# V' on eight small TensorE tiles, a cosine by one shifted sine, and other durations in the planner: a fused Nyström-attention and two-MLP kernel

## The chip, the cores and the metric

The program runs on one core of a Trainium2 chip, in one launch. The metric is the device time in microseconds (us). Three runs of the kernel before took 878.0, 874.71 and 877.42 us; their median is 877.42.

## The reference

Attention has 4 batches, 8 heads, 576 positions and 64 dimensions, with 32 landmarks per head (m). Its output, as 2304 tokens of 512 numbers, goes through two MLPs.

```python
q_lm, k_lm = segment means of q, k            # 32 per head
A, Bm, C = sm(q, k_lm), sm(q_lm, k_lm), sm(q_lm, k)
Z = Bm.T / (norm1 * norminf + 1e-6)
for _ in range(6):
    Z = 2 * Z - Z @ Bm @ Z
x = (A @ Z @ C @ v)                           # 2304 x 512
h = x @ w_in;  x = (h * cos(h)) @ w_out       # 512 -> 2048 -> 512
h = x @ w_in2; out = (max(h, 0) + alpha * min(h, 0)) @ w_out2
```

## The kernel before

**Algebra and tiles.** The first MLP's w_in is folded into the attention: per batch, W = Z C v (32 x 64 per head) is multiplied with w_in to V' = W w_in, and then h = A V'. Eight heads are four pairs p; two pairs make half c of a batch (c is 0 or 1), so V' is, per batch b, per block fb of 512 columns of w_in and per half c, one tile of 128 rows (4 heads of 32 landmarks) by 512. `vprime` (line 864) makes it: two matmuls in plain float32 (L885), each over all 128 rows (two heads of 64 dimensions) and 64 weight columns, the second on the other 64 columns of the array. The weights are block-diagonal: `put` (L857) writes W for both heads of a pair and multiplies what belongs to the other head with a mask of zeros. One ScalarE copy (L887) rounds V' from PSUM to its high part, one VectorE subtraction (L888) makes the low part. There are 4 x 4 x 2 = 32 such steps, here taken two by two (c = 0, 1) as 16 pairs.

**Ticks.** `tick` (line 909) is one block of 288 tokens by 128 columns of h, 128 in all. Six matmuls (L925) make h in one of two PSUM banks "h"; then the chain is ACT k = round(h/2pi) (L930), DVE u = h/2pi - k (L932), ACT sin(pi u) (L934), ACT square, times 2 (L935), DVE (1 - u)·h, which is h cos h (L936), ACT rounding to gh (L939), POOL or DVE gl (L940, by the helper at L323), and twelve matmuls (L952) into four banks "acc". The bank "h" is free again after L936.

**What else runs.** `unit` (line 523) makes A and C v of a half, `z_path` (line 757) the iteration for Z of a batch, both with the two PSUM banks "x" from the second batch on. `convert` (line 456) turns a float64 weight tile into float32 by three DVE operations (L467, L469, L471) after a load into one of three slots "raw". The second MLP (`btick`, `strassen`: L1238, L1319, L1283) follows the ticks, from about 460 us on.

**Order.** Nothing is ordered by hand. `Plan.go` (line 114) walks through all operations with an estimated duration of each (`pe`, `act`, `dve`, `pool`, lines 296 to 309), due times (`target`) and free buffers, picks what starts first, and so fixes the order on every engine; an operation that may run on two engines goes to the one that would end it first. Each engine then runs its list in that order, whatever the chip's real durations are.

Of the kernel before, what the change touches and what calls it, by code (L numbers as in the profile page):

```python
# [9 lines left out]
F32 = mybir.dt.float32  # L10
# [248 lines left out]
def kernel(  # L259
# [48 lines left out]
    def pool(n):  # L308
        return ("POOL", n / 480.0 + 0.15)
# [122 lines left out]
    kq = [view([P, 2, 2, 2, M], F32)(at_kq + 32 * M * p) for p in range(NP)]  # L432
# [3 lines left out]
    alpha_sb = keep.tile([P, NF], F32, name="alpha_sb")  # L436
    kqb = [[g.buf(None) for _ in range(2)] for _ in range(NP)]
# [85 lines left out]
    def unit(u, tu):  # L523
# [72 lines left out]
        if m == 0:  # L596
            pt = bank(1)
            for i, nm in enumerate(("kn", "qn")):
                a = nat[nm]
                if (KN["LM"] >> (2 * u + i)) & 1:  # L600
                    ls = atb(0, "ls", [P, P])
                    op(dve(1152), lambda e, a=a, ls=ls: nc.vector.tensor_reduce(
                        ls.t.rearrange("p (h d) -> p h d", h=2),
                        a.t.rearrange("p (h r d) -> p h d r", h=2, d=D), axis=AX.X, op=ALU.add), r=[a], w=[ls])
# [13 lines left out]
                op(pe(NR * P, 4), lm, r=[a], w=[pl])  # L618
                ls = atb(0, "ls", [P, P])
                op([act(128), dve(128)], lambda e, ls=ls, pl=pl: copy(e, ls.t[0:64], pl.t[0:64, 0:P]),  # L620
                   r=[pl], w=[ls])
                op(pe(128, 2), lambda e, i=i, ls=ls: nc.tensor.transpose(
                    pt.t[:, i * P:i * P + 64], ls.t[0:64], ident[0:64, 0:64]), r=[ls], w=[pt])
            for hh in range(2):
                sl = slice(64 * hh, 64 * hh + 64)

                def kw(e, sl=sl, hh=hh):
                    o = kq[p][sl, :, :, hh, :]
                    i = pt.t[sl, 0:256].rearrange("p (x y b m) -> p x y b m", x=2, y=2, b=2)[:, :, 0]
                    if e == "ACT":  # L630
                        nc.scalar.activation(o, i, AF.Copy, scale=1.0 / (8.0 * SEG))
                    else:
                        nc.vector.tensor_scalar_mul(o, i, 1.0 / (8.0 * SEG))
                op([dve(128), act(128)], kw, r=[pt], w=[kqb[p][0], kqb[p][1]])
        else:
            for i, t in enumerate((kt, qt)):
# [15 lines left out]
                for hh in range(2):  # L652
                    sl = slice(64 * hh, 64 * hh + 64)

                    def kw(e, sl=sl, hh=hh, i=i, lt=lt):
                        o = kq[p][sl, i, :, hh, :]
# [7 lines left out]
        def scores(dst, ch, which, t, bb, pp):  # L664
# [3 lines left out]
                lhsT=kq[pp][:, which, bb].rearrange("p h m -> p (h m)"),  # L668
# [5 lines left out]
        for ch in range(2):  # L674
# [5 lines left out]
            o1 = op(pe(n, 4), cs, r=[kt, kqb[p][1]], w=[sc[ch]] if ch else sc, after=[o1] if ch else [])  # L680
# [49 lines left out]
        for ch in range(2):  # L730
# [5 lines left out]
            o1 = op(pe(n, 4), asc, r=[qt, kqb[p][0]],  # L736
# [20 lines left out]
    def z_path(b, tz):  # L757
# [12 lines left out]
        def pbm(e):  # L770
            for p in range(g0, g0 + n):
                for bb in range(2):
                    for hh in range(2):
# [3 lines left out]
                            lhsT=kq[p][64 * hh:64 * hh + 64, 1, bb, hh, :],  # L777
                            rhs=kq[p][64 * hh:64 * hh + 64, 0, bb, hh, :],
# [40 lines left out]
        w_ = sb("wt", [P, 2, P])  # L819
# [39 lines left out]
        for i in range(2):  # L859
            wt[b, i] = w_  # L860
# [3 lines left out]
    def vprime(b, fb, c, target):  # L864
        g.ctx = f"{'vV'[b > 0]}{2 * fb + c}"
        if b > 1:
            wi = []
            for p in (2 * c, 2 * c + 1):
# [6 lines left out]
        else:  # L875
            wi = [wi1[fb, 2 * c], wi1[fb, 2 * c + 1]]
        w_ = wt[b, c]
        pv = psb("x")
        d = vv[b, fb, c] = v_tile()
        valloc.append((b, fb))  # L880
# [6 lines left out]
        op(act(512, True), lambda e: nc.scalar.activation(d.t[:, 0], pv.t, AF.Copy), r=[pv], w=[d], target=target + 0.8)  # L887
        op(dve(512), lambda e: nc.vector.tensor_tensor(d.t[:, 1], pv.t, f32(d.t[:, 0]), op=ALU.subtract),  # L888
           r=[pv], rw=[d], target=target + 1.5)
# [19 lines left out]
    def tick(s):  # L909
# [9 lines left out]
        def h1_mm(e):  # L919
# [8 lines left out]
        h1op[s] = op(pe(6 * CW), h1_mm, r=[vv[b, fb, 0], vv[b, fb, 1], *ah[b, 0], *ah[b, 1]], w=[hp], target=T,  # L928
                     after=[h1op[s - 1]] if s else [])
        op(act(CW, True), lambda e: nc.scalar.activation(k_.t, hp.t[:, 0:CW], AF.Copy, scale=INV2PI),  # L930
# [16 lines left out]
        for o in range(NK):  # L947
# [9 lines left out]
            y1op[s] = op(pe(3 * CW), y1_mm, r=[wh, wl, gh, gl], target=tick_time(s + LA) + 0.1 * o, **kw)  # L957
# [34 lines left out]
    def vgroup(b, fbs):  # L992
        for fb in fbs:
            for c in range(2):
                vprime(b, fb, c, tick_time(vfirst[b, fb]) - KN["VE"])
# [226 lines left out]
    def strassen(n, i, sg, js, X, Y):  # L1222
# [8 lines left out]
        def product(x, k, A, B):  # L1231
# [11 lines left out]
            return op(pe(6 * hw), mm, r=[a_, b_], hold=[(X, Y)[k // 2]], target=T, after=gates["h2"], **kw)  # L1243
# [23 lines left out]
    def btick(n, i, sg, jj):  # L1267
# [6 lines left out]
        if w < 512:  # L1274
            H = {}
            for D, A_, B_, x in ((X, "A11", "A12", 0), (Y, "A21", "A22", 2)):
# [9 lines left out]
                gates["h2"] = [op(pe(12 * w), mm, r=[y for z in ab for y in z], w=[D], target=T,  # L1286
# [7 lines left out]
        for j, x in ((ja, 0), (ja + 2 * NSG, 2)):  # L1294
# [18 lines left out]
            for t in range(w // P):  # L1313
# [8 lines left out]
                y2op[n, i] = op(pe(3 * 512), y2_mm, r=[wh, wl, gh, gl], target=btime(n, i + 1) + 4.6, **kw)  # L1322
# [62 lines left out]
```

## Time and profile before

| what | value |
|---|---|
| profiled execution | 876.8 us, span 875.0 us |
| median of 3 runs | 877.42 us |
| busy over the span: PE, DVE, ACT, POOL | 823.1, 642.5, 475.9, 200.0 us |
| mean granted TensorE clock | 0.974 |

The span is the time from the first to the last instruction. A busy TensorE (PE) means that a matmul was in flight; weight loads (PEld) overlap it. A clock of 1.00 is 2.4 GHz, one of 0.5 is 1.2 GHz; a stretch between them had both.

### The profile page before, as it was taken

What the parts mean: (1) busy time and instruction counts of PE and PEld (TensorE: products, weight loads), DVE (VectorE), ACT (ScalarE), POOL (GpSimd) and SP (SyncE); (2) the same over time, 40 slices, a digit from 0 to 9 for tenths busy, and PEclk for the clock granted to TensorE, in tenths of its full rate; (3) what the DMA queues carried; (4) which work ended last, traced back from release to release, by engine and by line L of the source; (5) the groups of instructions that cost most, each with busy time, mean ns of one, the idle gap of its engine ahead of it and who ended that gap; (6) DMA issues with size and microseconds to landing.
All of it is one profiled execution on the core that took longest, in us unless ns stands there. A gap on an engine that the chain in (4) does not pass through costs nothing.

```text
span 875.0 us, 16117 instructions
## 1 busy us (share of the span) xinstructions
PE 823.1 (94%) x6065; PEld 721.5 (82%) x6065; DVE 642.5 (73%) x1296; ACT 475.9 (54%) x1085; POOL 200.0 (23%) x221
## 2 busy tenths in 40 slices
PE   6658899999999999998999889999999999999997
PEld 4337678889788878877899779899999999999996
DVE  5978979986986789777978999865665566555563
ACT  4357647787866678566876443443344324433431
POOL 0325402334431332122511332200220012000110
PEclk9788799999999999999999999999999999999999
DMA  9474716676266935455463322130113011310231
GB/s 234 144 200 122 180 30 219 198 181 137 89 208 200 226 101 157 165 189 169 133 207 110 112 78 85 60 105 25 37 61 86 25 37 61 85 37 25 70 111 24
DMA packets 87901, 103.28 MB, mean 118 GB/s; under 512 B 35856, under 2 KB 62992, under 8 KB 87824
## 3 DMA queue, kind: packets, MB, share of 16 engines
q1 hardware_dynamic: 87824, 102.27, 40.6%
q8 instruction: 47, 0.77, 0.4%
q14 instruction: 30, 0.25, 0.1%
HBM read 79.96 MB, written 22.28 MB: 117 GB/s over the span
## 4 chain that ended last, share of the span: by engine, by line
PE 66%; DVE 15%; DMA 10%; ACT 3%; issue 3%; SPq 1%; DVEq 0%; ACTq 0%
PE acc L1319 20%; PE acc L952 14%; PE h L1238 9%; PE h L925 7%; PE x L1238 7%; DMA m<-in_moe_w_in_dram 5%; DVE m L323 3%; DMA m<-in_moe_w_out_dram 3%; PE x L885 2%; DVE m L469 1%; PE h L1283 1%; PE x L1283 1%; DVE m L471 1%; DMA m<-wi2d 1%; DVE m L936 1%
## 5 line engine op out<-in xcount | busy, mean ns | idle before, releaser
L952 PE MATMUL acc<-m,m 128*128 128x288 f32 x1536 | 239.1, 302 | 2.7 <-DVE m L323 2.2
L323 POOL TENSOR_TENSOR m<-m,m 128x288 fp32r<-128x288 f32 (+4 forms) x126 | 125.3, 1000 | 444.6 <-ACT m L939 193.3
L952 PEld LDWEIGHTS acc<-m,m 128*128 128x128 f32 x1536 | 214.8, 191 | 13.5 <-issue 5.5
L1319 PE MATMUL acc<-m,m 128*128 128x512 f32 x864 | 207.6, 391 | 0.7 <-DVE m L323 0.4
L323 DVE TENSOR_TENSOR m<-m,m 128x512 fp32r<-128x512 f32 (+3 forms) x274 | 174.0, 659 | 30.2 <-ACT m L1160 7.4
L1319 PEld LDWEIGHTS acc<-m,m 128*128 128x128 f32 x864 | 158.9, 189 | 31.5 <-DVE m L323 0.9
L925 PE MATMUL h<-m,m 128*128 128x288 f32 x768 | 131.2, 307 | 12.5 <-DVE m L936 11.1
L925 PEld LDWEIGHTS h<-m,m 128*128 128x128 f32 x768 | 110.7, 193 | 29.1 <-DVE m L936 18.6
L1238 PE MATMUL h<-m,m 128*128 128x256 f32 x768 | 107.8, 284 | 4.0 <-ACT m L318 4.0
L1307 ACT ACTIVATE m<-m 128x512 fp32r<-128x512 f32 (+1 forms) x80 | 46.3, 588 | 111.8 <-DVE m L1305 109.4
L1238 PEld LDWEIGHTS h<-m,m 128*128 128x128 f32 x768 | 101.0, 192 | 7.1 <-ACT m L318 4.8
L1238 PE MATMUL x<-m,m 128*128 128x256 f32 x576 | 80.9, 286 | 1.8 <-ACT m L318 1.8
L939 ACT ACTIVATE m<-m 128x288 fp32r<-128x288 f32 x128 | 56.2, 441 | 45.1 <-DVE m L936 41.3
L1261 DVE TENSOR_TENSOR m<-h,m 128x512 f32<-128x512 f32 x32 | 22.1, 690 | 78.1 <-ACT m L318 77.9
L1238 PEld LDWEIGHTS x<-m,m 128*128 128x128 f32 x576 | 74.0, 191 | 3.4 <-ACT m L318 2.0
L936 DVE SCALAR_TENSOR_TENSOR m<-m,h 128x288 f32<-128x288 f32 x128 | 56.8, 445 | 24.1 <-ACT m L935 23.8
L318 ACT ACTIVATE m<-h 128x256 f32<-128x256 f32 (+3 forms) x90 | 35.5, 395 | 63.2 <-PE h L1238 57.3
L930 ACT ACTIVATE m<-h 128x288 int32<-128x288 f32 x128 | 51.8, 406 | 31.8 <-PE h L925 30.9
L934 ACT ACTIVATE m<-m 128x288 f32<-128x288 f32 x128 | 55.7, 441 | 24.0 <-DVE m L932 23.4
L1071 ACT ACTIVATE m<-m 128x512 fp32r<-128x512 f32 x68 | 41.3, 627 | 45.2 <-PE h L1238 19.0
L932 DVE SCALAR_TENSOR_TENSOR m<-h,m 128x288 f32<-128x288 f32 x128 | 57.3, 448 | 6.2 <-ACT m L930 5.5
L935 ACT ACTIVATE m<-m 128x288 f32<-128x288 f32 x128 | 55.5, 439 | 2.3
(143 smaller groups left out, 864.8 us busy)
## 6 DMA issues: line engine op xcount, KB each, us to landing
m<-in_moe_w_in_dram SPq DMA_DIRECT2D x32, 512.0 KB, 4.9
m<-wi2d SPq DMA_DIRECT2D x56, 256.0 KB, 3.2
m<-in_moe_w_out_dram SPq DMA_DIRECT2D x24, 512.0 KB, 4.7
m<-w1d SPq DMA_DIRECT2D x32, 256.0 KB, 5.7
y1d<-m SPq DMA_DIRECT2D x24, 288.0 KB, 2.9
out_dram<-m SPq DMA_DIRECT2D x36, 128.0 KB, 2.4
w1d<-m SPq DMA_DIRECT2D x16, 256.0 KB, 5.6
wi2d<-m SPq DMA_DIRECT2D x16, 256.0 KB, 2.8
```

The source lines that it names most:

```text
L323: ENG[e].tensor_tensor(o, a, b, op=ALU.subtract)
L925: nc.tensor.matmul(out=hp.t[:, 0:CW], lhsT=w_[:, js], rhs=x[:, cs], start=(i == 0), stop=(i == 5))
L930: op(act(CW, True), lambda e: nc.scalar.activation(k_.t, hp.t[:, 0:CW], AF.Copy, scale=INV2PI), r=[hp], w=[k_], target=T + 0.8)
L932: op(dve(CW), lambda e: nc.vector.scalar_tensor_tensor(u.t, hp.t[:, 0:CW], INV2PI, k_.t, op0=ALU.mult, op1=ALU.subtract), r=[hp, k_], w=[u])
L934: op(act(CW), lambda e: nc.scalar.activation(u.t, u.t, AF.Sin, scale=math.pi), rw=[u], aset="sin")
L935: op(act(CW), lambda e: nc.scalar.activation(u.t, u.t, AF.Square, scale=math.sqrt(2.0)), rw=[u])
L936: op(dve(CW), lambda e: nc.vector.scalar_tensor_tensor(hc.t, u.t, 1.0, hp.t[:, 0:CW], op0=ALU.subtract, op1=ALU.mult, reverse0=True), r=[h ...
L939: op(act(CW), lambda e: nc.scalar.activation(gh.t, hc.t, AF.Copy), r=[hc], w=[gh, gl])
L952: nc.tensor.matmul(out=yg[o].t[:, 0:CW], lhsT=w_.t[:, sl], rhs=x.t, start=(j == ja and i == 0), stop=(j == jb and i == 2),)
L1238: nc.tensor.matmul(out=rv(k), lhsT=a_.t[:, p, c2, js], rhs=b_.t[:, q_, c2, 0:hw], start=(first and c2 == 0 and i == 0), stop=(c2 == 1 and ...
L1307: op(act(w), lambda e, m_=m_, gh=gh: nc.scalar.activation(gh.t[:, 0:w], m_.t[:, 0:w], AF.Copy), r=[m_], w=[gh, gl])
L1319: nc.tensor.matmul(out=ya[n][t].t, lhsT=gv(x_), rhs=r_.t, start=(st and k == 0), stop=(en and k == 2))
```

## The change

Three edits are made together.

**V'.** `vprime` now does both halves of a block fb in one step: eight matmuls, each of 64 rows (one head's dimensions) and 32 weight columns, on eight different tiles of the array. Half c writes PSUM bank `pv[c]`; head hh of pair bb stands in rows 64·hh, and its result in partitions 32·(2·bb + (hh xor c)). Without zero blocks the mask goes, and `put` is a plain copy that DVE or ACT may do. So that A's columns stand in the same order, the landmarks `kq` change their layout, and the two heads of a pair are swapped on A's side for c = 1.

**Cosine.** k = round(h/2pi + 1/4), u = h/2pi - k, and cos(h) = sin(2pi·u + pi/2), with the quarter turn as a per-partition bias from a tile `quarter`. The square is gone; the last DVE operation is a plain product.

**Planner.** The durations that it counts with are others (PE: per column 0.4258 ns instead of 0.4202, and 9 ns per matmul instead of 5 ns per step; POOL slower; ACT a little slower from SBUF; one reduction 2.06 instead of 1.27 us). Nothing else of its rules changes.

```diff
-    def pe(n, passes=1):
-        return ("PE", n * passes / 2380.0 + 0.005)
+    def pe(n, passes=1, k=1):
+        return ("PE", n * passes * 0.4258e-3 + 0.009 * k)
     def act(n, psum=False):
-        return ("ACT", n / 1200.0 + (0.05 if psum else 0.09))
+        return ("ACT", n * 0.8e-3 + 0.07 if psum else n * 0.835e-3 + 0.11)
     def pool(n):
-        return ("POOL", n / 480.0 + 0.15)
+        return ("POOL", n / 400.0 + 0.1)
...
             def put(e, bb=bb):
-                o = w_.t[:, :, 64 * bb:64 * bb + 64].rearrange("p i (h m) -> p h i m", h=2)
-                x = pw[bb].t[:, 0:n * M].rearrange("p (o i m) -> p o i m", o=1, i=n)
-                nv.tensor_tensor(o, x.to_broadcast([P, 2, n, M]), mask.to_broadcast([P, 2, n, M]), op=ALU.mult)
-            vop(128, put, r=[pw[bb]], w=[w_], target=tz)
+                copy(e, w_.t[:, :, bb], pw[bb].t[:, 0:n * M].rearrange("p (i m) -> p i m", i=n))
+            op([dve(64), act(64, True)], put, r=[pw[bb]], w=[w_], target=tz)
...
+        pv, d = [psb("x") for _ in range(2)], [v_tile() for _ in range(2)]
         def v_mm(e):
-            for bb in range(2):
-                sl = slice(64 * bb, 64 * bb + 64)
-                nc.tensor.matmul(out=pv.t[sl], lhsT=w_.t[:, c, sl], rhs=f32(wi[bb].t))
-        op(pe(512, 4), v_mm, r=[w_, *wi], w=[pv, d], target=target)
+            for c in range(2):
+                for bb in range(2):
+                    for hh in range(2):
+                        qd = 2 * bb + (hh ^ c)
+                        sl = slice(64 * hh, 64 * hh + 64)
+                        nc.tensor.matmul(
+                            out=pv[c].t[32 * qd:32 * qd + 32], lhsT=w_.t[sl, c, bb], rhs=f32(wi[2 * c + bb].t)[sl])
+        op(pe(512, 4, 12), v_mm, r=[w_, *wi], w=[*pv, *d], target=target)
...
-        op(act(CW, True), lambda e: nc.scalar.activation(k_.t, hp.t[:, 0:CW], AF.Copy, scale=INV2PI),
+        op(act(CW, True), lambda e: nc.scalar.activation(k_.t, hp.t[:, 0:CW], AF.Copy, scale=INV2PI, bias=0.25),
...
-        op(act(CW), lambda e: nc.scalar.activation(u.t, u.t, AF.Sin, scale=math.pi), rw=[u], aset="sin")
-        op(act(CW), lambda e: nc.scalar.activation(u.t, u.t, AF.Square, scale=math.sqrt(2.0)), rw=[u])
-        op(dve(CW), lambda e: nc.vector.scalar_tensor_tensor(
-            hc.t, u.t, 1.0, hp.t[:, 0:CW], op0=ALU.subtract, op1=ALU.mult, reverse0=True), r=[hp, u], w=[hc],
+        op(act(CW), lambda e: nc.scalar.activation(u.t, u.t, AF.Sin, scale=2.0 * math.pi, bias=quarter), rw=[u], aset="sin")
+        op(dve(CW), lambda e: nc.vector.tensor_tensor(hc.t, u.t, hp.t[:, 0:CW], op=ALU.mult), r=[hp, u], w=[hc],
```

**Where it moves instructions.** In the lists below m with a number is a tile in SBUF, and h, x and acc are the PSUM banks. After the change the lines stand a little lower: L885 is L886, L925 is L930, L952 is L955, L590 is L592, L839 is L841, L743 and L749 are L745 and L751.

First place: TensorE at a V' pair in the middle of the ticks (last batch, block 2). Before:

```order
L952 MATMUL acc<-m_541,m_698 128x288 x2
L952 MATMUL acc<-m_541,m_699 128x288
L885 MATMUL x<-m_204,m_450 64x512 x2
L885 MATMUL x<-m_280,m_450 64x512 x2
L925 MATMUL h<-m_884,m_509 128x288 x3
L925 MATMUL h<-m_1189,m_578 128x288 x3
L952 MATMUL acc<-m_541,m_742 128x288 x2
```

With the change:

```order
L955 MATMUL acc<-m_555,m_709 128x288 x2
L955 MATMUL acc<-m_555,m_710 128x288
L886 MATMUL x<-m_198,m_479 32x512 x4
L886 MATMUL x<-m_235,m_479 32x512 x4
L955 MATMUL acc<-m_555,m_762 128x288 x2
L955 MATMUL acc<-m_555,m_763 128x288
L930 MATMUL h<-m_819,m_542 128x288 x3
L930 MATMUL h<-m_1173,m_543 128x288 x3
```

Four matmuls of 64 columns have become eight of 32; the place among h and acc is nearly the same.

Second place: TensorE at the second V' pair of the first batch (its half c = 0 is m_468). Before:

```order
L925 MATMUL h<-m_453,m_473 128x288
L925 MATMUL h<-m_452,m_473 128x288
L885 MATMUL x<-m_468,m_450 64x512 x2
L590 MATMUL x<-m_69,m_154 128x128 x3
L925 MATMUL h<-m_445,m_463 128x288
L925 MATMUL h<-m_446,m_463 128x288
```

With the change:

```order
L930 MATMUL h<-m_499,m_485 128x288
L930 MATMUL h<-m_498,m_485 128x288
L886 MATMUL x<-m_452,m_479 32x512 x4
L886 MATMUL x<-m_510,m_479 32x512 x4
L930 MATMUL h<-m_382,m_484 128x288
L930 MATMUL h<-m_383,m_484 128x288
```

Before, half c = 1 (m_558) came only after two more ticks' h (12 matmuls). Now both halves stand ahead of these two ticks.

Third place: DVE in the first batch's iteration for Z (its steps are the 128x192 rows). Before:

```order
L746 TENSOR_REDUCE m_172<-m_172 128x18
L839 SCALAR_TENSOR_TENSOR m_69<-m_69,h 128x192
L747 TENSOR_SCALAR m_172<-m_172 128x18
L471 SCALAR_TENSOR_TENSOR m_204<-m_154,m_204 128x512
L467 TENSOR_SCALAR m_280<-m_154 128x512
L839 SCALAR_TENSOR_TENSOR m_69<-m_69,h 128x192
L469 SCALAR_TENSOR_TENSOR m_280<-m_154,m_280 128x512
```

With the change:

```order
L751 TENSOR_TENSOR m_191<-m_191 128x576
L841 SCALAR_TENSOR_TENSOR m_69<-m_69,h 128x192
L754 STREAM_TRANSPOSE m_191<-m_191 128x576
L740 STREAM_TRANSPOSE m_191<-acc 128x320
L740 STREAM_TRANSPOSE m_191<-acc 128x256
L841 SCALAR_TENSOR_TENSOR m_69<-m_69,h 128x192
L745 TENSOR_REDUCE m_191<-m_191 128x18
L469 TENSOR_SCALAR m_235<-m_153 128x512
L841 SCALAR_TENSOR_TENSOR m_69<-m_69,h 128x192
L323 TENSOR_TENSOR m_191<-m_191 128x576
```

A multiplication and a subtraction 576 wide, which POOL did here before, stand between the steps of the iteration. In the whole program the list of DVE has five of L749's eight operations more than before, four more of the 512-wide L1099, and 14 more subtractions gl; POOL has these fewer.

## Rows read from the trace of the kernel before

**Rows 1.** The page, part 1: busy time, share and instructions of each engine.

```profile
PE 823.1 (94%) x6065; PEld 721.5 (82%) x6065; DVE 642.5 (73%) x1296; ACT 475.9 (54%) x1085; POOL 200.0 (23%) x221
```

**Rows 2.** Busy time by stage: the stage (us), its length, busy us (count) per engine.

```profile
core 0: us, PE busy (x) PEld busy (x) DVE busy (x) ACT busy (x) POOL busy (x), PEclk, DMA share, GB/s
0.00:43.00 43.00, 27.82 (x336) 18.33 (x338) 30.61 (x79) 18.25 (x37) 8.77 (x15) 0.85 0.70 188
43.00:110.00 67.00, 51.33 (x326) 39.08 (x323) 55.73 (x107) 44.55 (x99) 25.82 (x29) 0.84 0.67 168
110.00:460.00 350.00, 340.81 (x2867) 298.11 (x2867) 280.29 (x625) 249.89 (x597) 104.70 (x121) 1.00 0.56 163
460.00:540.00 80.00, 75.22 (x494) 69.87 (x494) 73.47 (x136) 38.65 (x83) 20.49 (x14) 0.96 0.31 97
540.00:870.00 330.00, 327.91 (x2050) 296.12 (x2049) 202.36 (x353) 124.32 (x272) 40.23 (x43) 1.00 0.19 57
```

**Rows 3.** The same for short stretches, columns as in rows 2.

```profile
20.00:40.00 20.00, 13.27 (x254) 8.08 (x254) 18.93 (x57) 7.93 (x19) 5.65 (x4) 0.84 0.45 129
...
490.00:500.00 10.00, 8.26 (x43) 6.34 (x41) 10.00 (x15) 4.64 (x10) 3.68 (x3) 1.00 0.27 84
...
520.00:530.00 10.00, 7.70 (x48) 7.29 (x46) 8.66 (x18) 4.13 (x9) 0.12 (x1) 0.83 0.45 134
```

**Rows 4.** Timeline of PE at a V' pair: start us, length us, line, operands, count.

```profile
131.74 0.55 PE L952 MATMUL acc<-m,m 128*128 128x288 f32 x3
132.22 1.94 PE L885 MATMUL x<-m,m 128*64 128x512 f32 x8
134.09 1.06 PE L925 MATMUL h<-m,m 128*128 128x288 f32 x6
```

**Rows 5.** Line L885 from 100 to 425 us: duration ns min/median/max, first and last start.

```profile
L885 PE MATMUL x<-m,m x112: 592/592/643, 126.2 to 419.2; 128*64 128x512 f32 x112
```

**Rows 6.** Timeline of PE: steps on tiles of 64 and 32 rows by 32 columns.

```profile
239.09 0.33 PE L775 MATMUL x<-m 64*32 64x32 f32 x16
...
248.73 0.53 PE L826 MATMUL x<-m 32*32 32x96 f32 x16
```

**Rows 7.** Timeline of PE at the start: V' of the first batch; in brackets idle before, releaser.

```profile
40.58 3.60 PE L885 MATMUL x<-m,m 128*64 128x512 f32 x8 [0.16 <-DVE m L857]
...
56.10 1.04 PE L885 MATMUL x<-m,m 128*64 128x512 f32 x2 [3.19 <-DVE m L471]
57.58 1.95 PE L885 MATMUL x<-m,m 128*64 128x512 f32 x2 [0.43 <-DVE m L471]
```

**Rows 8.** Groups by line and shape: busy us, mean ns | idle before, releasers.

```profile
L936 DVE SCALAR_TENSOR_TENSOR m<-m,h 128x288 f32<-128x288 f32 x128 | 56.8, 445 | 24.1 <-ACT m L935 23.8
L935 ACT ACTIVATE m<-m 128x288 f32<-128x288 f32 x128 | 55.5, 439 | 2.3
L318 ACT ACTIVATE m<-x 128x256 f32<-128x256 f32 x32 | 12.2, 383 | 15.4 <-PE x L1238 15.1
L972 DVE TENSOR_TENSOR m<-acc,m 128x288 f32<-128x288 f32 x16 | 6.9, 452 | 1.2 <-PE acc L952 0.9
L688 ACT ACTIVATE m<-x,m 128x256 f32<-128x256 f32 x6 | 2.8, 467 | 0.0
```

**Rows 9.** Waits of PE, 100 to 460 us: total us, times, longest.

```profile
PE h L925 <- DVE m L936: 6.6, 11, 1.5
```

**Rows 10.** Groups by line and shape on DVE, columns as in rows 8.

```profile
L469 DVE SCALAR_TENSOR_TENSOR m<-m,m 128x512 int32<-128x512 int32 x56 | 41.6, 747 | 0.5
L1099 DVE TENSOR_TENSOR m<-m,m 128x512 f32<-128x512 f32 x10 | 8.2, 822 | 0.0
L752 DVE STREAM_TRANSPOSE m<-m 128x576 f32<-128x576 f32 x8 | 6.1, 763 | 0.2 <-POOL m L749 0.2
L323 DVE TENSOR_TENSOR m<-m 128x576 f32<-128x576 f32 x3 | 3.7, 1229 | 0.0
L749 DVE TENSOR_TENSOR m<-m 128x576 f32<-128x576 f32 x1 | 0.8, 757 | 0.0
```

More of the change, by code (lines that the diff above doesn't have):

```diff
@@ L431 @@
         nc.vector.memset(mask[64 * hh:64 * hh + 64, hh], 1.0)
-    kq = [view([P, 2, 2, 2, M], F32)(at_kq + 32 * M * p) for p in range(NP)]
+    kq = [view([P, 2, 4, M], F32)(at_kq + 32 * M * p) for p in range(NP)]
     for p in range(NP):
@@ L436 @@
     alpha_sb = keep.tile([P, NF], F32, name="alpha_sb")
+    quarter = keep.tile([P, 1], F32, name="quarter")
+    nc.vector.memset(quarter, math.pi / 2)
     kqb = [[g.buf(None) for _ in range(2)] for _ in range(NP)]
@@ L601, in unit @@
                     ls = atb(0, "ls", [P, P])
-                    op(dve(1152), lambda e, a=a, ls=ls: nc.vector.tensor_reduce(
+                    op(("DVE", 2.06), lambda e, a=a, ls=ls: nc.vector.tensor_reduce(
                         ls.t.rearrange("p (h d) -> p h d", h=2),
@@ L627, in kw @@
                 def kw(e, sl=sl, hh=hh):
-                    o = kq[p][sl, :, :, hh, :]
-                    i = pt.t[sl, 0:256].rearrange("p (x y b m) -> p x y b m", x=2, y=2, b=2)[:, :, 0]
+                    o = kq[p][sl, :, 1:3] if c and hh == 0 else kq[p][sl, :, 0:4:3] if c else kq[p][sl, :, hh:4:2]
+                    i = pt.t[sl, 0:256].rearrange("p (x y b m) -> p y b x m", x=2, y=2, b=2)[:, 0]
                     if e == "ACT":
@@ L667, in scores @@
                 out=dst.t[64 * bb:64 * bb + 64, 0:n],
-                lhsT=kq[pp][:, which, bb].rearrange("p h m -> p (h m)"),
+                lhsT=kq[pp][:, bb, 2 * which:2 * which + 2].rearrange("p h m -> p (h m)"),
                 rhs=t.t[:, CH[ch][0]:CH[ch][1], bb, :],
@@ L679, in cs @@
                     scores(sc[ch], ch, 1, kt, bb, p)
-            o1 = op(pe(n, 4), cs, r=[kt, kqb[p][1]], w=[sc[ch]] if ch else sc, after=[o1] if ch else [])
+            o1 = op(pe(n, 4, 4), cs, r=[kt, kqb[p][1]], w=[sc[ch]] if ch else sc, after=[o1] if ch else [])
             op(dve(n), lambda e, ch=ch, n=n: nc.vector.reduce_max(mx.t[:, ch:ch + 1], sc[ch].t[:, 0:n], axis=AX.X),
@@ L854, in put, with vprime @@
             def put(e, bb=bb):
-                o = w_.t[:, :, 64 * bb:64 * bb + 64].rearrange("p i (h m) -> p h i m", h=2)
-                x = pw[bb].t[:, 0:n * M].rearrange("p (o i m) -> p o i m", o=1, i=n)
-                nv.tensor_tensor(o, x.to_broadcast([P, 2, n, M]), mask.to_broadcast([P, 2, n, M]), op=ALU.mult)
-            vop(128, put, r=[pw[bb]], w=[w_], target=tz)
-        for i in range(2):
-            wt[b, i] = w_
+                copy(e, w_.t[:, :, bb], pw[bb].t[:, 0:n * M].rearrange("p (i m) -> p i m", i=n))
+            op([dve(64), act(64, True)], put, r=[pw[bb]], w=[w_], target=tz)
+        wt[b] = w_
     vv, vload = {}, {}
-    def vprime(b, fb, c, target):
-        g.ctx = f"{'vV'[b > 0]}{2 * fb + c}"
+    def vprime(b, fb, target):
+        g.ctx = f"{'vV'[b > 0]}{fb}"
         if b > 1:
             wi = []
-            for p in (2 * c, 2 * c + 1):
+            for p in range(NP):
                 f = sb("wi", [P, 512], I32)
@@ L875, in vprime @@
         else:
[L876 to L880, printed above, removed]
-        def v_mm(e):
-            for bb in range(2):
-                sl = slice(64 * bb, 64 * bb + 64)
-                nc.tensor.matmul(out=pv.t[sl], lhsT=w_.t[:, c, sl], rhs=f32(wi[bb].t))
-        op(pe(512, 4), v_mm, r=[w_, *wi], w=[pv, d], target=target)
-        op(act(512, True), lambda e: nc.scalar.activation(d.t[:, 0], pv.t, AF.Copy), r=[pv], w=[d], target=target + 0.8)
-        op(dve(512), lambda e: nc.vector.tensor_tensor(d.t[:, 1], pv.t, f32(d.t[:, 0]), op=ALU.subtract),
-           r=[pv], rw=[d], target=target + 1.5)
+            wi = [wi1[fb, p] for p in range(NP)]
+        w_ = wt[b]
+        pv, d = [psb("x") for _ in range(2)], [v_tile() for _ in range(2)]
+        valloc.extend([(b, fb)] * 2)
+        def v_mm(e):
+            for c in range(2):
[6 more added lines that the diff above has]
+        op(pe(512, 4, 12), v_mm, r=[w_, *wi], w=[*pv, *d], target=target)
+        for c in range(2):
+            vv[b, fb, c] = d[c]
+            op(act(512, True), lambda e, c=c: nc.scalar.activation(d[c].t[:, 0], pv[c].t, AF.Copy), r=[pv[c]],
+               w=[d[c]], target=target + 0.8)
+            op(dve(512), lambda e, c=c: nc.vector.tensor_tensor(
+                d[c].t[:, 1], pv[c].t, f32(d[c].t[:, 0]), op=ALU.subtract), r=[pv[c]], rw=[d[c]], target=target + 1.5)
     JG = KN["JG"]
@@ L993, in vgroup @@
         for fb in fbs:
-            for c in range(2):
-                vprime(b, fb, c, tick_time(vfirst[b, fb]) - KN["VE"])
+            vprime(b, fb, tick_time(vfirst[b, fb]) - KN["VE"])
     FH = JG // 4
@@ L1242, in product @@
             kw = {"w": [reg[k]]} if first else {"rw": [reg[k]]}
-            return op(pe(6 * hw), mm, r=[a_, b_], hold=[(X, Y)[k // 2]], target=T, after=gates["h2"], **kw)
+            return op(pe(6 * hw, k=6), mm, r=[a_, b_], hold=[(X, Y)[k // 2]], target=T, after=gates["h2"], **kw)
         def keep(k, d, i):
@@ L1285, in mm @@
                                     start=(k + c2 + q_ == 0), stop=(k * c2 * q_ == 2))
-                gates["h2"] = [op(pe(12 * w), mm, r=[y for z in ab for y in z], w=[D], target=T,
+                gates["h2"] = [op(pe(12 * w, k=12), mm, r=[y for z in ab for y in z], w=[D], target=T,
                                   after=gates["h2"])]
```

16 lines of the change are left out of this document (8 added, 8 removed).

## The prediction

> **What bounds the kernel now.** I read the page's busy times first, then the same by stage, then the TensorE timeline at the places that the change touches, then the waits. Over the span PE is busy 94%, DVE 73%, ACT 54%, POOL 23% [rows 1]; that average hides five stages [rows 2]. From 110 to 460 us, where most ticks run, PE is busy 340.8 of 350.0 us at full clock while DVE has 80% and ACT 71%: there a microsecond of PE work is a microsecond of time, and what else could be won is the 9.2 us in which PE is idle. From 540 to 870 us (second MLP) PE is busy 327.9 of 330.0 us, and no instruction there changes its kind. Before 110 us it is different: PE is idle for 15.2 and 15.7 us of the two first stages at a clock of 0.85 and 0.84, while DVE, with the unit chains and the weight conversions, is busy 18.9 of 20 us from 20 to 40 us [rows 3]. From 460 to 540 us PE is idle 4.8 us and DVE busy 92% [rows 2]; in 490 to 500 and 520 to 530 DVE is full or nearly so and PE is at 8.3 and 7.7 of 10 us [rows 3]. So the change has to be costed in three places: PE work in the ticks, DVE's order at the start, DVE's load at the change of stages.
>
> **V'.** The first two batches' first pairs run in the slow start; after 100 us there are 112 records of L885 [rows 5], eight to a pair [rows 4], so 14 pairs. One pair takes PE from 132.22 to 134.09, 1.87 us [rows 4]. Its eight records are four rounds of two tiles: (1.94 - 0.592)/3 = 0.449 us from round to round [rows 4, 5] (a float32 matmul of 512 columns leaves two records). Eight tiles need two rounds instead of four, which saves 2 x 0.449 = 0.90 us. Six more starts in a round cost something: 16 records on small tiles take 0.33 us in all [rows 6], so a start costs at most 0.33/16 = 0.021 us and six at most 0.12 us. The saving is thus 0.78 to 0.90 us a pair; I take 0.86 us, since the starts of one round mostly lie beside the round before: 14 x 0.86 = **-12.0 us** (10.9 to 12.6). The switch into other tile shapes stays, once per pair. The eviction (two ACT copies, two DVE subtractions) is the same work; both banks "x" are taken at once, which two adjacent halves did before, too.
>
> That tiles of different rows really run side by side shows in L826: 16 records of 96 columns on tiles of 32 rows end within 0.53 us [rows 6], all into one PSUM bank. A round of 512 columns takes 0.449 us, so 96 columns take 0.084; one after the other 16 would need 1.35 us, two by two 0.67, four by four 0.34 us, and only the last leaves room for a record's tail of 0.592 - 0.449 = 0.14 us. L775, on tiles of 64 by 32 like the new ones, has 0.33 us [rows 6], between what four by four (0.25) and two by two (0.37) would give, and decides little. The Trainium skill, "TensorEngine Tiling (Array Packing)", section Restrictions and Gotchas, states that different row tiles cannot access the same PSUM bank simultaneously; the change puts two row tiles into each of its two banks. By that rule the four tiles of a bank would run in two turns, and the 12.0 us would be 0. The L826 row speaks against it, so I keep it as a rival with a small chance.
>
> **Cosine.** 128 square operations of 439 ns leave ACT, 56 us [rows 8]. ACT is not the bound in any stage [rows 2], so that by itself gives nothing. The sine now has a bias per partition: an exponential with such a bias (and a running sum) takes 467 ns for 256 columns, a plain copy of that size 383 ns [rows 8], so up to 84 ns more, or nothing. The product on DVE replaces one of 445 ns by an operation whose nearest row has 452 ns [rows 8]: no change. A tick's chain from h to the free bank gets shorter by 0.355 to 0.44 us. PE waited for that chain's end 11 times in 100 to 460 us, 6.6 us in all [rows 9]. Cutting 0.36 us from each gives 4 us at most; I take **-3 us** (0 to -6.6), because a wait that ends earlier often only meets the next one.
>
> **The planner at the start.** Two 576-wide operations come from POOL to DVE between the steps of the first iteration for Z (1.23 and 0.76 us on DVE) and a transpose (0.76), two conversion steps (0.75 at most each) and two PSUM copies (under 0.76 each) come ahead of its end [rows 10]: 3.5 to 6 us, where DVE has 1.07 us of 20 free [rows 3]. So the first V' (40.58 us [rows 7]) starts about 4.6 us later. Part of that is work done ahead that is missing later; about 24 us of DVE's 110 are idle [rows 2] and can take some up; and a V' pair at the half clock takes 3.60 us [rows 7], of which two of four rounds, 1.8 us, go. I take **+3 us** for what is left when PE becomes the bound (0 to +7).
>
> **The planner later.** DVE gets 14 more subtractions gl and five of the 576-wide products, beside PE in a stage where DVE has 70 us free [rows 2]: nothing. If that cover were gone they would cost 14 x 0.45 + 5 x 0.76 = 10 us. Of the 512-wide sums, four more go to DVE, 4 x 0.822 = 3.3 us [rows 10], some of them in the full stretches around 500 us [rows 3]: **+1 us** (0 to 3.3). Elsewhere PE's order differs in small swaps of h and acc, whose stalls I cannot price; they are why the range is wider than the terms.
>
> **Sum.** The profiled execution has 876.8 us, 0.6 less than the median of 877.42: 876.8 - 12.0 - 3 + 3 + 1 = 865.8, **866 us**. With the terms' ends the forecast's own range is 859 to 873.
>
> **Rivals.**
> - Only four tiles run side by side. No row before shows more than four at once, so the second bank's tiles could start only when the first four begin their second pass: three rounds instead of two, a saving of 0.43 us a pair, 6.0 in all: 876.8 - 6 - 3 + 3 + 1 = 872 us. For it: nothing shows eight. Against it: all eight have different places in the array. 10%.
> - Row tiles take turns at a PSUM bank: four rounds as before, 876.8 - 3 + 3 + 1 = 878 us. L826 speaks against it, and only its 32-row tiles do so clearly. 6%. It is what the Trainium skill's "TensorEngine Tiling (Array Packing)" states.
> - V' does what it should, but DVE gives most of it back: the start keeps its whole 7 us, the stage change 3.3, and no wait of rows 9 gets shorter: 876.8 - 12 + 7 + 3 = 875 us. For it: DVE is at 95% from 20 to 40 us [rows 3] and only gets more. Against it: its idle time before 110 us. 13%.
> - Slower: the second V' pair of the first batch holds up the start. Before, half c = 1 waited for its last converted weights until 57.58 us [rows 7], and PE had done two more ticks by then; now these ticks' h and nine transposes of the next unit stand behind the whole pair in PE's list. Between the first V' and that last half lay 17.0 us (40.58 to 57.58). If DVE's new order has the last two weight tiles converted only behind the next unit's chain, and the wait reaches that whole 17 us again with PE standing, the time is 876.8 - 12 + 17 + 3 = 885 us. It decides from a slip of 12 us on. Against it: the same eight tiles have to be converted either way, and DVE has idle time there [rows 2]. 7%.
>
> **How the numbers follow.** The forecast has 64%. A measurement of this kernel tells about 0.5% from no change: below 873.0 is faster, above 881.8 slower. Faster: 0.62 of the forecast, 0.06 of the four-tile case, 0.04 of the DVE case, together 0.72. Same: 0.02 + 0.04 + 0.09 + 0.06 = 0.21. Slower: 0.07. The range from 857 to 878 takes in the forecast with 2 us for unpriced reordering below it, and the rivals up to 878; some 0.15 is outside.
>
> **What would show it.** Right: L886 rows of 16 records and about 1.1 us in the timeline, with the next matmul about 1.0 us after the first; PE's busy time near 811 us; DVE's sum up by about 15 us, ACT's down by 45 to 56; fewer waits of h for the product on DVE; the first V' at 43 to 46 us; the second MLP's first matmul some 10 us earlier. A row of 1.5 or 1.9 us would show three or four rounds. The prediction is wrong if PE's idle time in the ticks grows over 9 us, or if PE's load becomes dense only after 117 us.

## The result, and the profile after

The kernel with the change takes 890.47 us, the median of 4 runs (887.34 to 892.75); the kernel before, beside it on the same chip, 876.07. The ratio is 1.0146 (95% interval 1.0114 to 1.0177): 1.5% slower, where 866 us was forecast and the range ended at 878. The profiled execution has 892.75 us and a span of 890.6.

First the page's busy times, then the stages as in [rows 2]:

```profile
PE 816.5 (92%) x6193; PEld 718.8 (81%) x6193; DVE 648.9 (73%) x1321; ACT 435.0 (49%) x960; POOL 172.4 (19%) x192
```

```profile
43.00:110.00 67.00, 47.00 (x361) 34.92 (x361) 57.28 (x109) 34.75 (x75) 24.54 (x29) 0.88 0.61 161
110.00:460.00 350.00, 324.04 (x2907) 285.45 (x2905) 275.96 (x619) 212.53 (x480) 94.46 (x107) 0.99 0.56 160
540.00:870.00 330.00, 328.23 (x2059) 297.06 (x2058) 214.05 (x379) 127.67 (x280) 38.08 (x36) 1.00 0.21 61
```

TensorE has less to do, as foreseen, and is idle instead: 26.0 us of the 350 between 110 and 460 us, where it was 9.2 [rows 2]. Each of the pieces nevertheless does what it was costed at. The timeline of TensorE at the V' pair that answers to [rows 4]:

```profile
129.61 1.06 PE L955 MATMUL acc<-m,m 128*128 128x288 f32 x6
130.60 1.09 PE L886 MATMUL x<-m,m 64*32 64x512 f32 x16
131.62 1.60 PE L955 MATMUL acc<-m,m 128*128 128x288 f32 x10
```

From the first V' matmul to the next other one are 1.02 us instead of 1.87: 0.85 us saved for a pair. The eight tiles run side by side: in the trace the eight first records start 6.6 ns apart (130.599 to 130.646), the eight second ones 0.454 us later. And the groups of the cosine by line, with the TensorE groups that wait for it:

```profile
L939 ACT ACTIVATE m<-m,quarter 128x288 f32<-128x288 f32 x128 | 67.8, 534 | 59.3 <-DVE m L937 58.4
L940 DVE TENSOR_TENSOR m<-m,h 128x288 f32<-128x288 f32 x128 | 56.8, 448 | 20.8 <-ACT m L939 20.2
L930 PE MATMUL h<-m,m 128*128 128x288 f32 x768 | 129.9, 305 | 21.7 <-DVE m L940 17.2 <-ACT m L891 3.1 <-DVE m L893 1.3
```

The square is gone; the sine with its bias takes 534 ns where the one without took 441, in this row of the kernel before:

```profile
L934 ACT ACTIVATE m<-m 128x288 f32<-128x288 f32 x128 | 55.7, 441 | 24.0 <-DVE m L932 23.4
```

So the chain is 0.35 us shorter. Yet h waits longer for the product that frees its bank. These are the three largest waits of TensorE's matmuls after the change, from 110 to 460 us (total us, times, longest):

```profile
PE h L930 <- DVE m L940: 11.2, 11, 2.4
PE acc L955 <- DVE m L320: 4.2, 3, 2.9
PE x L668 <- DVE m L320: 2.1, 2, 1.3
```

The first had 6.6 us before [rows 9]. The other two are copies out of PSUM that the planner gave to VectorE (L320); before, TensorE waited 0.8 us in all for such copies. The two kinds together make 10.1 of the 16.8 us by which TensorE's idle time grew.

Where time is lost is told by when each tick's first ScalarE operation starts (us, read from the traces; the last two columns are experiments told of below):

```
tick    before   after   e6_tiles_old_order   e15_both_landing_323
0         46.9    52.7         47.5                  49.1
12       100.7   100.4        101.3                  91.3
16       131.2   135.2        130.9                 131.6
40       194.0   201.6        195.3                 188.4
64       275.4   283.6        276.7                 275.0
96       381.7   395.5        388.3                 376.9
127      471.1   486.8        476.7                 458.0
```

The 5.8 us lost at the first tick are made good by tick 12; tick 16 is 4.0 us late again. The loss then builds up over the ticks, to 15.7 us at the last, and what follows the ticks takes as long as before. What took the place of TensorE's work is in the chain that ended last. This is its share by line from 110 to 460 us, first of the kernel before, then of the kernel after:

```profile
by line: PE acc L952 29.2%; PE h L925 15.5%; DMA m<-in_moe_w_in_dram 9.7%; PE x L885 5.6%; DMA m<-in_moe_w_out_dram 4.3%; issue 4.1%; DVE m L323 3.7%; DVE m L936 2.4%; DMA m<-wi2d 2.2%; DVE m L932 2.1%; PE x L590 2.0%; PE x L666 1.9%; DVE m
```

```profile
by line: DMA m<-in_moe_w_in_dram 12.5%; PE acc L955 12.2%; DMA m<-in_moe_w_out_dram 7.4%; PE h L930 6.4%; issue 5.9%; DVE m L323 5.0%; DVE m L471 4.9%; DVE m L473 4.5%; DVE m L940 3.8%; DVE m L937 3.4%; DVE m L469 3.3%; SPq L550 2.1%; DMA m
```

Here stands what the prediction overlooked. In a stretch in which TensorE is "busy" 97% of the time, its lines in the first row come to 54% of the chain (29.2 + 15.5 + 5.6 + 2.0 + 1.9); 14.0% are loads of float64 weights, on which VectorE's conversion waits. After, TensorE's matmuls for acc and h have fallen from 44.7% to 18.6%, the loads of weights stand at 19.9%.

### The profile page after: what moved, and what is told of

Read it like the earlier page. It is cut to its first block, busy times and chain, and to the rows that moved or that the text cites. A ratio compares the mean times of both kernels' runs of the same rounds, so it can differ in the third digit from the quotient of the medians.

```text
span 890.6 us, 16315 instructions
## 1 busy us (share of the span) xinstructions
PE 816.5 (92%) x6193; PEld 718.8 (81%) x6193; DVE 648.9 (73%) x1321; ACT 435.0 (49%) x960; POOL 172.4 (19%) x192
## 4 chain that ended last, share of the span: by engine, by line
PE 51%; DVE 22%; DMA 14%; ACT 6%; issue 3%; SPq 3%; POOL 0%; ACTq 0%; DVEq 0%; POOLq 0%
PE acc L1321 20%; PE h L1240 9%; PE x L1240 7%; PE acc L955 6%; DMA m<-in_moe_w_in_dram 5%; DMA m<-in_moe_w_out_dram 5%; DVE m L323 4%; PE h L930 3%; DVE m L471 3%; DVE m L473 3%; DMA m<-in_q_dram 2%; DVE m L940 2%; DVE m L469 2%; DVE m L937 2%; PE x L1285 1%
## 5 line engine op out<-in xcount | busy, mean ns | idle before, releaser
L955 PE MATMUL acc<-m,m 128*128 128x288 f32 x1536 | 241.9, 302 | 11.3 <-DVE m L323 5.7
L955 PEld LDWEIGHTS acc<-m,m 128*128 128x128 f32 x1536 | 214.5, 190 | 30.9 <-issue 9.1
L323 DVE TENSOR_TENSOR m<-m,m 128x512 fp32r<-128x512 f32 (+4 forms) x293 | 180.0, 638 | 43.3 <-ACT m L942 17.3
L323 POOL TENSOR_TENSOR m<-m,m 128x288 fp32r<-128x288 f32 (+4 forms) x107 | 108.4, 1020 | 514.0 <-ACT m L942 191.1
L930 PE MATMUL h<-m,m 128*128 128x288 f32 x768 | 129.9, 305 | 21.7 <-DVE m L940 17.2
L930 PEld LDWEIGHTS h<-m,m 128*128 128x128 f32 x768 | 109.9, 191 | 32.5 <-DVE m L940 22.1
L939 ACT ACTIVATE m<-m,quarter 128x288 f32<-128x288 f32 x128 | 67.8, 534 | 59.3 <-DVE m L937 58.4
L940 DVE TENSOR_TENSOR m<-m,h 128x288 f32<-128x288 f32 x128 | 56.8, 448 | 20.8 <-ACT m L939 20.2
L318 ACT ACTIVATE m<-x 128x384 f32<-128x384 f32 (+4 forms) x78 | 31.4, 416 | 30.0 <-PE x L1240 17.3
```

The source lines that it names most:

```text
L318: nc.scalar.activation(o, i, AF.Copy)
L323: ENG[e].tensor_tensor(o, a, b, op=ALU.subtract)
L930: nc.tensor.matmul(out=hp.t[:, 0:CW], lhsT=w_[:, js], rhs=x[:, cs], start=(i == 0), stop=(i == 5))
L940: op(dve(CW), lambda e: nc.vector.tensor_tensor(hc.t, u.t, hp.t[:, 0:CW], op=ALU.mult), r=[hp, u], w=[hc], target=T + 2.6)
L955: nc.tensor.matmul(out=yg[o].t[:, 0:CW], lhsT=w_.t[:, sl], rhs=x.t, start=(j == ja and i == 0), stop=(j == jb and i == 2),)
```

## The experiments

Theories at the start: **A**, the new durations make an order that stalls; **B**, the new instructions stall by themselves; **C**, any other order costs time here. The ratios are to the kernel before, run beside each on the same chip. Runs are named by their labels, which are also the headings of the quoted expectations.

### Parts of the change: e1 to e4

e1_old_durations is the whole change with the planner's durations of before:

```diff
-        return ("PE", n * passes * 0.4258e-3 + 0.009 * k)
+        return ("PE", n * passes / 2380.0 + 0.005)
```

(and the same for ACT, POOL and the one reduction).

> The change with the planner's old durations: eight tiles and shifted sine stay. Theory A (the new durations make an order that stalls PE): the stalls go and the two savings stay, 876 - 12 - 0 to 3 = 861 to 866 us. Theory B (the sine, now 534 ns with its per-partition bias instead of 441, or the V' step that needs both banks at once, makes the stalls): 884 to 892 us, as the whole change. Theory C (any edit makes another order, and the old one was the lucky end of many trials): anywhere in 862 to 885 us, with PE's idle time in 110 to 460 us over 15 us.

Measured: 879.29 us, 1.0004 (0.9984 to 1.0024). e2_durations_alone is the kernel before with the new durations:

```diff
-        return ("PE", n * passes / 2380.0 + 0.005)
+        return ("PE", n * passes * 0.4258e-3 + 0.009 * k)
```

> The kernel before with the planner's new durations alone; V' and cosine stay as before. Theory A: the change without its 12 us of saved PE work, 890 + 12 = 900 us or somewhat less, 890 to 905. Theory B: as before, 872 to 880 us. Theory C: slower than before by 0 to 25 us, with no fixed relation to the other runs.

Measured: 895.39 us, 1.0193 (1.0178 to 1.0208). With no instruction changed the durations cost 1.9%, and in the whole change 1.4%. So the slowdown is theirs. But e1, without them, gains nothing at all. e3_tiles_alone has only the tiles of V', e4_sine_alone only the shifted sine, both with the old durations.

> The kernel before with V' on eight tiles alone; old cosine, old durations. Theory A: 876 - 12 = 864 us, 862 to 867. Theory B, if the V' step makes the stalls: 876 us or more; if the sine does: 864. Theory C: 862 to 880 us.

> The kernel before with the shifted sine alone; V' and durations as before. Theory A: 870 to 877 us (no PE work saved, a chain shorter by 0.35 us). Theory B, if the sine makes the stalls: 885 us or more. Theory C: 868 to 885 us.

Measured: 886.3 us, 1.0094 (1.0074 to 1.0114), and 880.74 us, 1.0031 (1.0002 to 1.0059). Alone neither part gains: e3 is slower than both together, and e4's interval overlaps that of e1. The parts don't add; each comes with an order of its own.

### The same order: e5 and e6

In e5_both_old_order all instructions are issued in the order of before: V' as two steps of four tiles each, the square a step of the planner that issues nothing. e6_tiles_old_order does that with the tiles alone (the new layout of `kq` and the plain copy in `put` go with them and are left out here):

```diff
             for bb in range(2):
-                sl = slice(64 * bb, 64 * bb + 64)
-                nc.tensor.matmul(out=pv.t[sl], lhsT=w_.t[:, c, sl], rhs=f32(wi[bb].t))
+                for hh in range(2):
+                    qd = 2 * bb + (hh ^ c)
+                    sl = slice(64 * hh, 64 * hh + 64)
+                    nc.tensor.matmul(out=pv.t[32 * qd:32 * qd + 32], lhsT=w_.t[sl, c, bb], rhs=f32(wi[bb].t)[sl])
```

> Eight tiles and shifted sine, with the order of every engine as in the kernel before: the planner still counts with the old steps and durations (two V' steps of two matmuls, a square that issues nothing, the old copy on DVE), and only what is issued is new. If the loss of the other versions comes from the new order alone: 876 - 12 - 0 to 4 = 860 to 865 us, PE idle in 110 to 460 us at most 10 us. If the new instructions themselves stall the engines (longer sine, both banks): 876 us or more.

> Eight tiles alone, in the order of the kernel before. Order is the cause: 862 to 866 us, against the 886 us of the same instructions in the order that the planner makes for them. Otherwise: 880 us or more.

Measured: 882.61 us, 1.0066 (1.0038 to 1.0094), and 882.0 us, 1.0045 (1.0022 to 1.0067). So even in the old order the saved TensorE time buys nothing, and e5's chain, 0.35 us shorter in each tick, nothing either. The expectation of e5 had put such a result under B. The busy times of e6 from 110 to 460 us (columns as in [rows 2]), and its waits there (us in total, times, longest), say where the saved time goes:

```profile
110.00:460.00 350.00, 328.27 (x2942) 289.60 (x2941) 275.82 (x619) 244.62 (x587) 103.12 (x120) 1.00 0.55 160
```

```profile
PEld h L925 <- DVE m L936: 19.1, 22, 2.9
PE h L925 <- DVE m L936: 15.1, 18, 2.7
DVE m L467 <- DMA m<-in_moe_w_in_dram: 12.0, 7, 2.8
DVE m L467 <- DMA m<-in_moe_w_out_dram: 8.3, 7, 1.8
```

In the kernel before the four waits are 13.4, 6.6, 8.6 and 5.5 us. TensorE arrives earlier and waits for the product L936, which stands in VectorE's list behind conversions that wait for weights. The largest loss of e6's ticks, 3.8 us, lies between ticks 68 and 72. The chain there in e6 (start, us, what):

```profile
281.75 0.61 DVE m L471
282.37 0.02 issue
282.38 0.32 SPq L494
282.70 0.05 issue
282.75 0.55 SPq L548
...
285.43 6.67 DMA m<-in_moe_w_in_dram
292.10 0.02 issue
292.12 0.04 DVE m L467
```

A loop without TensorE: the conversion ends (L471), SP, which has waited for it, issues its store (L494), then four loads of k (L548), and only then the next load of weights; 6.67 us later it lands, and VectorE, at a standstill for 2.85 us, begins the next conversion. In the kernel before the same load was issued at 282.98 and took 5.02 us. Against B speaks that no new instruction waits here, and that the same instructions gain in other orders (e15 and e18 below).

### The order alone: e7 and e8

Each is the kernel before with one number of the planner changed by about half a per cent or by 10 ns; no instruction differs.

```diff
-        return ("PE", n * passes / 2380.0 + 0.005)
+        return ("PE", n * passes / 2370.0 + 0.005)
```

```diff
-        return ("ACT", n / 1200.0 + (0.05 if psum else 0.09))
+        return ("ACT", n / 1200.0 + (0.05 if psum else 0.10))
```

> The kernel before with one number of the planner changed by 0.4% (PE's 2380 columns per us become 2370). No instruction changes, only the order. If any other order than the one before costs 5 to 20 us: 881 to 895 us. If only particular new durations do harm: 874 to 880 us.

> The kernel before with ACT's fixed cost from SBUF at 0.10 instead of 0.09 us in the planner, and nothing else. Any other order costs: 881 to 895 us. Only particular durations do harm: 874 to 880 us.

Measured: 882.94 us, 1.0057 (1.0037 to 1.0078), and 895.5 us, 1.0200 (1.0162 to 1.0238). 10 ns in an estimate cost as much as all of the new durations. C holds in a weaker form: a new order moves the time by amounts as large as all terms of the prediction, but not every new order costs time (e16 below, 0.9985).

### What the ticks wait for: e9 and e10

Both keep the order of before. e9_v_twice issues each V' matmul twice, the second time over the first result:

```diff
-            for bb in range(2):
+            for bb in (0, 1, 0, 1):
```

> The kernel before in its own order, with the four matmuls of each of the 16 V' tile pairs issued twice: 16 x 1.9 us = 30 us more of TensorE work, on no other engine. If the ticks are bound by TensorE's work (the prediction's reading), 14 of the 16 pairs count: +26 us, some 904 us beside 878. If TensorE only waits at another engine's pace there, its idle time takes part of it: the trace of the kernel before shows 95 us between matmul starts beyond their columns in ticks 16 to 127, so +0 to +13 us. A theory in which TensorE's time is free would say +0.

Measured: 898.2 us, 1.0220 (1.0193 to 1.0246). 30 us more work (the busy time of L885 in the trace grew by 28.9 us, from 34.8 to 63.7) cost 19, between the two cases of the expectation: TensorE does count, upwards. e10_short_dve leaves out the reduction of the cosine's argument; VectorE only scales k there:

```diff
-        op(dve(CW), lambda e: nc.vector.scalar_tensor_tensor(
-            u.t, hp.t[:, 0:CW], INV2PI, k_.t, op0=ALU.mult, op1=ALU.subtract), r=[hp, k_], w=[u])
+        op(dve(CW), lambda e: nc.vector.tensor_scalar(
+            u.t, k_.t, 0.25, None, op0=ALU.mult), r=[hp, k_], w=[u])
```

> The kernel before in its own order, where the reduction of the argument (k is subtracted from the scaled h, from PSUM, 448 ns) is left out: VectorE only scales k, in SBUF, so the cosine is of the wrong argument. VectorE has 128 x some 0.2 us = 25 us less to do and each tick's chain is as much shorter; TensorE and ScalarE do the same. If VectorE's queue sets the pace of the ticks: -15 to -22 us, some 857 to 863 beside 878. If TensorE does: 0. If the landing of transfers does, for which VectorE waits at the conversion of weights: 0 to -5, and those waits (18 us before) grow.

Measured: 876.48 us, 0.9977 (0.9955 to 0.9998). The expectation had the size wrong: the operation takes 389 ns instead of 448, 7.5 us in all, not 25. Some 2 of them come back, and the waits of VectorE's conversion for transfers grow from 18.1 to 20.7 us over the span, as the expectation's third case has it. So no engine alone sets the pace: adding to TensorE costs two thirds, taking from it (e6) gives nothing.

### A landing nearer to the measured one: e11, e12, e15 to e18

The planner takes a 512 KB load of weights for landed 0.65 + 1.46 + 0.93 = 3.04 us after its issue, if no other transfer is ahead of it. The median from issue to landing is 4.9, in this row of the kernel before (each load's size, then that median):

```profile
m<-in_moe_w_in_dram SPq DMA_DIRECT2D x32, 512.0 KB, 4.9
```

One line of `Plan.go` was changed, to 2.43 in e11 and e12, to 3.23 in the others. It holds for every transfer, not for weights alone:

```diff
-                o.end = dma_free + 0.93
+                o.end = dma_free + 3.23
```

e11_late_landing and e16_landing_323 are the kernel before with it, e12_both_late_landing and e15_both_landing_323 both edits with the old durations, e18_tiles_landing_323 the tiles alone, e17_change_landing_323 the whole change, new durations and all.

> The kernel before, with one number of the planner changed: a transfer counts as landed 2.43 us after its bytes have gone, not 0.93; no instruction is changed, all are ordered anew. VectorE then should wait less for weights that have not landed (18 us before). If these waits are the price of every order here: -5 to -15 us, 863 to 873. If the order before is good by chance, as the other runs with a new order and no new instruction suggest: +2 to +18 us whatever becomes of those waits.

> Both edits of the change with the planner's old durations of engines, and transfers that count as landed 2.43 us after their bytes have gone. Without the latter 879.3. If late weights are what held back that kernel (27 us of waits for them): 864 to 872, faster than both. If a new order costs whatever it costs by chance: 876 to 895.

> Both edits, the planner's old durations, and a transfer that counts as landed 3.23 us after its bytes have gone. If what made the run with 2.43 us fast is that VectorE does not wait for weights: 870 to 878 again, with under 8 us of these waits. If that run was a lucky order: 876 to 895.

> The kernel before with the landing of 3.23 us: the partner of the run with both edits and 3.23. If the edits are worth something: 4 to 12 us above that one. If late weights are what costs time here: 868 to 876. If each order costs what it costs by chance: 876 to 895.

> The whole change, new durations too, with the landing of 3.23 us. Without it 890.5; with the old durations and this landing 866.4. If the new durations make a worse order on their own account: 876 to 885. If what they spoil is the moment at which weights land: 864 to 872.

> The tiles of V' alone, old durations, landing of 3.23 us. If the tiles carry the gain, as the prediction's terms have it (12 of 15 us): 866 to 870. If the cosine's shorter chain does: 873 to 877. If each order is a draw of its own, beside which the edits are small: anywhere from 866 to 885.

Measured:

| landing | no edit | tiles | both edits | both and new durations |
|---|---|---|---|---|
| 0.93 | 1 | 1.0094 (e3) | 1.0004 (e1) | 1.0146 (after) |
| 2.43 | 1.0040 (1.0016 to 1.0065) | | 0.9961 (0.9942 to 0.9980) | |
| 3.23 | 0.9985 (0.9960 to 1.0009) | 0.9915 (0.9887 to 0.9944) | 0.9866 (0.9826 to 0.9906) | 0.9878 (0.9834 to 0.9922) |

e15, 866.41 us, is faster than both kernels, and so is the whole change with this one number: 868.85. The waits of e15's conversion for transfers, over the whole span, are down to one row (e17 has 2.2 us of them, e18 none), and the chain from 110 to 460 us is again TensorE's:

```profile
DVE m L469 <- DMA m<-in_moe_w_in_dram: 0.7, 1, 0.7
```

```profile
by line: PE acc L955 38.4%; PE h L930 19.6%; DVE m L323 3.8%; issue 2.6%; DVE m L940 2.6%; DMA m<-in_moe_w_in_dram 2.5%; PE x L828 2.4%; PE x L886 2.4%; DVE m L473 2.1%; DVE m L937 2.1%; DVE m L471 2.1%; PE x L668 2.0%; DMA m<-y1d 1.7%; DVE
```

```profile
110.00:460.00 350.00, 339.03 (x3077) 306.52 (x3076) 289.37 (x634) 231.50 (x517) 104.86 (x117) 1.00 0.58 168
```

e16, without the edits, has hardly any of these waits either (1.2 us) and gains nothing that can be told from zero: there TensorE's own work is what is left. e6 took away TensorE's work and kept the waits: nothing. Only both together pay. That is how two chains look that end at nearly the same time. It is a reading: that these orders are better draws for some other reason is not excluded, though all four orders with one or both edits and a later landing are faster than the kernel before, and no other new order is by more than its interval. One thing doesn't fit: e11 has only 6.6 us of these waits, and is 0.4% slower than the kernel before; in its chain stands a single piece of 10.74 us (at 242.89) in which an engine waited for nothing that the profile shows.

### Pairs: e13 and e14

These are the partners, with both edits, of e7 and e8: the change to 2370 and the one to 0.10 on top of e1.

> Both edits, the planner's durations of before but TensorE's 2380 columns per us as 2370: the partner of the run in which that number alone was changed in the kernel before (882.9 beside 878.2). If the edits are worth something whatever the order: 874 to 880. If they are worth nothing: anywhere from 872 to 895, as often above 882.9 as below.

> Both edits, the planner's durations of before but 0.10 us instead of 0.09 as ScalarE's fixed part: the partner of the run in which that number alone was changed (895.5 beside 878.2). If the edits are worth something whatever the order: 880 to 892. If they are worth nothing: as often above 895.5 as below.

Measured: 877.85 us, 0.9991 (0.9969 to 1.0012), and 881.98 us, 1.0045 (1.0024 to 1.0066). With them there are six settings of the planner, each with and without the two edits:

| the planner's numbers | without | with both edits | the edits |
|---|---|---|---|
| of before | 1 | 1.0004 | +0.0% |
| the new durations | 1.0193 | 1.0146 | -0.5% |
| TensorE 2370 | 1.0057 | 0.9991 | -0.7% |
| ScalarE 0.10 | 1.0200 | 1.0045 | -1.6% |
| landing 2.43 | 1.0040 | 0.9961 | -0.8% |
| landing 3.23 | 0.9985 | 0.9866 | -1.2% |

The edits help in five of six, by 0.8% in the mean, 7 us; six pairs that spread so much leave some 2 to 12 us for that mean (an estimate from their spread). The column without them spreads over 2.2%, and no order in it is faster than that of before by more than its interval: a change that is judged in one new order is compared with a good draw.

## Why the prediction was wrong

**What bounds the kernel.** The step that failed is "there a microsecond of PE work is a microsecond of time". It was read from a busy share of 97%; but busy only means that a matmul is in flight, not that with less work the next one would come earlier. e6 shows it at the same order: busy time in that stretch fell from 340.8 to 328.3 us and no time was won. The Trainium skill, "Perfetto Trace Analysis", section Identifying the Most-Contended Engine, states that the matmul busy share is not a good measure of how close one is to roofline, because pipelined instructions look smaller in the trace. These runs agree that the share misleads (97% busy, 54% of the chain), but here it looked too large. The chain of waits, with 14% of weights on their way, was there to be read and was left out.

**The sign that was named.** That TensorE's idle time in the ticks grows over 9 us was one of the signs put down for a wrong prediction, and it is what happened (26.0 us). Of the signs for a right one only those of the V' row held: TensorE's busy time is 816.5 us instead of 811, VectorE's sum is up by 6.4 us instead of 15, ScalarE's down by 40.9 instead of 45 to 56, and the waits for the product did not get fewer. Of the rivals, the one in which VectorE gives most of the gain back had the right engine, but put it at the start and at the change of stages, not in every tick.

**V'.** The term was right as work: 0.85 us a pair measured, 0.86 put. Both rivals about the tiles are refuted by the 6.6 ns between the starts: neither four at a time nor turns at a bank. "TensorEngine Tiling (Array Packing)" of the Trainium skill, Restrictions and Gotchas, does not agree with the trace here: in each bank two row tiles write side by side, and the rounds take 0.454 us as for one. As time the 12 us were 0 to 6: nothing in the old order (e6), less than nothing in a new one (e3), 0.7% with a later landing (0.9985 to 0.9915).

**Cosine.** The bias costs 93 ns, a little over the 84 at most; the chain became 0.35 us shorter, just under the prediction's 0.355 to 0.44. The Trainium skill, "ScalarE: Activation LUTs", in the section What ACT_TABLE_LOAD costs, gives about 93 ns for each per-partition operand, and 534 against 441 ns agrees; it would have given a better price than the exponential's row. That "a wait that ends earlier often only meets the next one" came true with the old landing: there the sine is worth nothing (e4 1.0031, e5 against e6); with the later one e15 against e18 has 0.5%, the 3 us put and a little more, but their intervals overlap.

**The planner at the start.** The first V' starts at 46.38 us, 5.8 later, near the end of the range for it. That is made good by tick 12, so of +3 us nothing is left there. Between ticks 12 and 16 some 4.3 us are lost again, where the chain holds two loads of w_out (5.20 us from 90.98 and 4.75 us from 99.48); whether they go back to the start is not shown. The slower rival's place, the second V' pair at 57 us, was not it, either: that pair does wait for a conversion (12 of its 16 records start at 55.85, 1.8 us after the other four), and no tick is late for it at tick 12.

**The planner later.** The step that sized this at +1 us, and put the rest into "small swaps of h and acc, whose stalls I cannot price", is the one that decided the sign. The new order costs 1.4% in the change (e1 against after) and 1.9% alone (e2), 12 to 17 us. In both kernels with the new durations the share of weights on their way in the chain from 110 to 460 us is about 20% (e2: 20.4) instead of 14.0; 6% of 350 us are 21 us. With the later landing the same durations cost 0.1% (e17 against e15). That speaks for the moment at which weights are there as what they spoil, and doesn't settle it: e1, with the old durations, has 21.2% and loses nothing against the kernel before, and e8 is as slow as e2 with 13.4% for the loads of w_in. The conversion's waits for transfers over the span are 18.9 us in the kernel after, hardly more than the 18.1 before, and 28.0 in e1. Neither the share nor these waits alone give the time.

**The sum.** The ends given for the four terms add up to 857.6 and 876.2 us, not to the 859 and 873 that stand there as the forecast's own range. The measured time lies outside both. By the runs, the two edits gave nothing where 15 us were put (e1), and the new durations cost 12 us where 4 were (e1 against after).

**What stays open.** Which feature makes one order faster than another when both wait little for weights (e11 against e16), or much (e1 against e2), is not settled, and single orders differ by more than an edit is worth. The mean of six pairs, 7 us, is therefore a better figure for the edits than any one pair.

## What to carry to other kernels

Before calling a busy engine the bound, read the chain of waits over that stretch: where it holds much else (here 14% transfers), work saved on the engine is given back to a second chain that ends nearly as late, and both have to be shortened. Where a planner fixes the order, change a number by a hair and run the old kernel again: that spread (here 2%) is the least that a forecast must allow, and an edit is judged by pairs under several settings. Correcting some estimates of a planner and leaving the worst of them (here the landing of transfers, 3.0 us for 4.9) can make its order worse.

## What the runs showed of the hardware

Eight tiles of 64 rows and 32 columns, with two different row tiles writing to one PSUM bank (on different partitions), start 6.6 ns apart and run side by side at the pace of one: 0.454 us for a pass of 512 columns. A load of 512 KB took 4.9 us in the median, but 6.67 at one place and 5.02 at the same place in the kernel before, with the same loads ahead of it: a fixed estimate cannot hit both.
